# Laying q and k six tokens to a partition, and re-planning the first units, in a fused windowed-attention and gated-FFN kernel

## The chip, the cores and the metric

The kernel runs on one core of one Trainium2 chip. The core has a matrix engine (TensorE, PE in the profile, with its weight loads shown as PEld), VectorE (DVE), ScalarE (ACT), GpSimd (POOL), a queue engine (SP), and 16 DMA engines that move data between the chip's memory (HBM) and SBUF. TensorE writes its sums to PSUM banks, from which ACT or DVE must fetch them. The metric is the device time of one execution in microseconds (us); lower is better.

## The reference

Inputs in fp32: q, k and v of 8 batches x 8 heads x 576 tokens x 64, and three weights.

```python
scores = scale * np.matmul(q, k.transpose(0, 1, 3, 2))      # per batch and head, 576 x 576
rel = pos[:, None] - pos[None, :]
mask = (rel >= 0) & (rel < 64)                              # each token sees itself and the 63 before it
attn = softmax(where(mask, scores, -1e9)); x = attn @ v     # -> 4608 tokens x 512
gate = np.maximum(x @ w_gate, 0.0); val = x @ w_val         # 512 -> 1536
out = (gate * val) @ w_out                                  # 1536 -> 512, fp32
```

## The kernel before, in words

The attention is cut into 24 **units** of 192 tokens, three to a batch (all 8 heads at once); the FFN into 12 **tiles** of 384 tokens, two units each. Everything is multiplied in fp16.

*A unit's steps.* `u_cast` (L194) makes fp16 of fp32 q and k where they were loaded as fp32. `u_trans` (L205) turns them with 32x32 block transposes on DVE into kT and qT (head dimension on partitions). `u_st` (L244) computes scores, 32 matmuls on quarters of the array, into four PSUM banks `st`, one for each pair of heads. `u_exp` (L265) does four exponentials on ACT into `p`; `u_mask` (L270) multiplies them by the band mask on DVE (units 0 and 1 get the mask as a large negative bias instead: `u_bias`, L218, four matmuls a unit). `u_pv` (L275) multiplies by v. From unit 1 on it is the wide form (L294): v's tile holds 64 columns of ones beside each head's 64 columns of v, so that one matmul gives the weighted values and the row sums. `u_copy` (L310, ACT, two copies of 64x768) and `u_sum` (L320, DVE, two transposes of 64x768) take values and sums out of the PSUM tile `pv`. `u_back` (L331: reciprocal, transpose) and `u_norm` (L339: a product) write the fp16 input `xt` of the tile.

*A tile's steps.* `hidden` (L377): for each of 12 blocks f of 128 hidden columns, four matmuls with the gate weights wg, then four with the value weights wv (a "group" is four matmuls); ACT applies relu to the first into `r_sb` (L385), DVE multiplies that by the second into `g_sb` (L388). `output` (L426) or `output_by_rows` (L435): 36 matmuls with wo (L412), three copies by ACT (L419) and three stores issued by SP. The PSUM pool `f_ps` has four banks (tag `h`), shared in turn by the groups, the outputs and unit 0's `st` and `pv`. The pool `a_ps` is one tile of four banks, used in turn by every other `st` and `pv`.

*Loads.* q and k of batches 0 and 1 (units 0 to 5) come as fp32, in pieces of 32 partitions: each partition takes pairs of consecutive tokens, so that runs of 512 bytes are contiguous. `qk_load` (L159) issues them on SP, half of the first ones on ACT. Those of batch 1 are held back by `qk_gate` (L181), a memset on POOL. From batch 2 on, one `qk_load` for a whole batch issues eight DMAs on the POOL queue, which convert to fp16 on the way. v (`v_load`, L186, two DMAs a unit) and the weights (`w_load`, L132) always take the POOL queue and convert on the way. POOL also casts k and q of most units 2 to 5 and k of unit 0 (L203).

*What sets the order.* Nothing is reordered by a scheduler. `Weaver` (L16) is a heap of (time, function): attention steps and loads are entered by `plan_unit` (L347) with planned times, and issued into the engines' queues while `hidden` and `output` advance a clock by the ideal length of their matmuls. The planned times set only the *order* in each in-order engine queue; on the chip semaphores hold each instruction until its data is there. `ready(n)` issues planned steps until unit n-1 is normalized. DMAs on the POOL queue go round eight semaphores, so the ninth issue waits for the first landing, and so on.

*Order of the work* (L444 on): load k, then q; 22 matmuls on zeros (`heat`, L228); constants; units 0 and 1; tile 0 on 192 tokens for f 0 to 3, twice, then on 384 tokens for f 4 to 11; tile 1's first half on 192 tokens; tile 0's output; tile 1's second half; its output; then tiles 2 to 11, each with two later units woven in.

Of the kernel before, what the change touches and what calls it, by code (L numbers as in the profile page):

```python
# [42 lines left out]
def kernel(  # L43
# [10 lines left out]
    nc = tc.nc  # L54
# [24 lines left out]
    a_ps = ctx.enter_context(tc.tile_pool(name="a_ps", bufs=1, space=bass.MemoryType.PSUM))  # L79
# [13 lines left out]
    def constants():  # L93
        for kT in kTs:
            nc.vector.memset(kT[:, :, 0:64], 0.0)
        nc.vector.memset(v16s[0][0:64, 0], 0.0)
        for i in range(UB):
            nc.vector.memset(v16s[i][64 if i == 0 else 0:, 0, :, 64:128], 1.0)
            nc.vector.memset(v16s[i][:, 1, :, 64:128], 1.0)
        nc.vector.memset(ones, 1.0)  # L100
        nc.vector.memset(ones0, 1.0)
        nc.vector.memset(ones0[0:64], 0.0)
# [4 lines left out]
        for band, lo, hi in ((mask[:, 0], 64, -1), (mask[:, 1], 0, 63), (ident, 0, 0)):  # L107
# [9 lines left out]
        nc.vector.tensor_scalar(bias, mask, 30000.0, -30000.0, MUL, mybir.AluOpType.add)  # L117

# [11 lines left out]
    w_done = set()  # L130

    def w_load(wt, src, f0, f1):  # L132

        sr = src.rearrange("(c p) n -> p c n", p=128)
        if wt is wo:
            dst, part = wo[:, f0:f1], sr[:, f0:f1]
        else:
            ns = slice(128 * f0, 128 * f1)
            dst, part = wt[:, :, ns], sr[:, :, ns]
        nc.gpsimd.dma_start(dst, part)  # L140
        w_done.update((wt.name, f) for f in range(f0, f1))

    def w_need(wt, f):
        while (wt.name, f) not in w_done:
            W.pop()

# [3 lines left out]
    def qk_tiles(b):  # L150
        for name in ("k", "q"):
            direct = b >= 2
            nat = a_in.tile([128, 2, UB, 3, 128], FP16 if direct else FP32,
                            name=name + ("h" if direct else "n"), bufs=2)
            for i in range(UB):
                units.setdefault(UB * b + i, {})[name + ("16" if direct else "")] = nat[:, :, i]
                units[UB * b + i][name + "nat"] = nat

    def qk_load(b, blocks=None, names="kq", two=False):  # L159

        for name, src in (("k", k), ("q", q)):
            if name not in names:
                continue
            nat = units[UB * b + UB - 1][name + "nat"].rearrange("p h u m e -> p h (u m) e")
            for i in range(G):
                g = i // 2 + 2 * (i % 2)
                rows = slice(32 * g, 32 * g + 32)
                eng = nc.gpsimd if b >= 2 else nc.scalar if two and g >= G // 2 else nc.sync
                if blocks is None:
                    eng.dma_start(  # L170
                        nat[rows].rearrange("p h m e -> p (h m) e"),
                        src[b, 2 * g:2 * g + 2].rearrange("h (m i j) d -> i (h m) (j d)", i=32, j=2))
                else:
                    m0, m1 = blocks
                    for h in range(2):
                        eng.dma_start(  # L176
                            nat[rows, h, m0:m1],
                            src[b, 2 * g + h, 64 * m0:64 * m1].rearrange(
                                "(m i j) d -> i m (j d)", i=32, j=2))

    def qk_gate(b):  # L181

        for name in ("k", "q"):
            nc.gpsimd.memset(units[UB * b][name + "nat"].rearrange("p h u m e -> p (h u m) e")[:, :, 0:1], 0.0)
# [9 lines left out]
    def u_cast(u, name):  # L194
# [3 lines left out]
        c16 = d[name + "16"] = a_16.tile([128, 2, 3, 128], FP16, name=name + "16")  # L198
        src = d[name]
        if u < 3 and (u, name) not in ((0, "k"), (2, "k")):  # L200
# [334 lines left out]
```

The softmax here doesn't subtract the row's maximum and nothing guards it: scores larger than these inputs give would overflow.

## Time and profile before

| | us |
|---|---|
| median of three runs (range) | 351.43 (350.75 to 351.93) |
| the profiled execution: its time | 352.04 |
| its span, first to last instruction | 350.3 |
| busy: PE / DVE / ACT / POOL | 334.8 / 232.9 / 180.4 / 89.2 |
| first FFN matmul starts | 19.19 |
| tile 1's second half starts | 62.23 |
| tile 2's first group starts | 82.48 |
| last output copy starts | 346.55 |

The profile's page gives busy times by engine; the span in 40 slices of 8.76 us (PE busy tenths, the clock granted to TensorE in tenths, the share of DMA engines busy, GB/s that they moved, counted in bytes as they land); the chain of work that ended last, followed back from the end; and groups of like instructions with busy time, mean length, and idle time ahead of them with what ended it. The timeline lists instructions in order of time: start, length, engine, line, operation, and in brackets the idle time before it and who ended it. A run of matmuls is shown with its pipeline's depth, so the distance between starts, not the length, is its cost.

### The profile page before, as it was taken

What the parts mean: (1) busy time and instruction counts of PE and PEld (TensorE: products, weight loads), DVE (VectorE), ACT (ScalarE), POOL (GpSimd) and SP (SyncE); (2) the same over time, 40 slices, a digit from 0 to 9 for tenths busy, and PEclk for the clock granted to TensorE, in tenths of its full rate; (3) what the DMA queues carried; (4) which work ended last, traced back from release to release, by engine and by line L of the source; (5) the groups of instructions that cost most, each with busy time, mean ns of one, the idle gap of its engine ahead of it and who ended that gap; (6) DMA issues with size and microseconds to landing.
All of it is one profiled execution on the core that took longest, in us unless ns stands there. A gap on an engine that the chain in (4) does not pass through costs nothing.

```text
span 350.3 us, 7421 instructions
## 1 busy us (share of the span) xinstructions
PE 334.8 (96%) x2910; PEld 200.6 (57%) x2910; DVE 232.9 (66%) x432; ACT 180.4 (52%) x346; POOL 89.2 (25%) x129
## 2 busy tenths in 40 slices
PE   8579989999999999999999999999999999999995
PEld 3467674865555655655665664664664664664652
DVE  6487756697766766766766766766776777675430
ACT  2745552746565464465564564563663663663331
POOL 5944022835110710134120720216110100000000
PEclk9859999999999999999999999999999999999999
DMA  6999999999833992429615894409906501001002
GB/s 189 165 204 191 213 196 95 186 94 189 91 25 99 90 97 92 32 18 184 81 11 112 63 111 107 30 3 158 121 2 104 49 2 60 33 0 62 30 2 90
DMA packets 95508, 32.21 MB, mean 92 GB/s; under 512 B 76017, under 2 KB 90865, under 8 KB 95473
## 3 DMA queue, kind: packets, MB, share of 16 engines
q0 software_dynamic: 80048, 17.57, 57.5%
q1 hardware_dynamic: 13760, 13.38, 13.3%
q10 hardware_dynamic: 1664, 0.79, 0.8%
q8 instruction: 23, 0.38, 0.4%
q14 instruction: 13, 0.10, 0.1%
HBM read 39.85 MB, written 9.44 MB: 141 GB/s over the span
## 4 chain that ended last, share of the span: by engine, by line
PE 70%; DMA 13%; DVE 8%; issue 4%; POOL 3%; SPq 1%; ACT 0%; DVEq 0%; POOLq 0%
PE h L398 37%; PE op L412 24%; PE pv L303 5%; DMA kn<-in_k_dram 5%; DVE g_sb L388 5%; DMA wv<-in_moe_w_val_dram 4%; DMA qn<-in_q_dram 4%; PE st L256 3%; DVE sT L329 3%; SPq L176 1%; POOL v L192 1%; DVE rT L335 1%; POOL wg L140 1%; POOL k L203 0%; POOL wv L140 0%
## 5 line engine op out<-in xcount | busy, mean ns | idle before, releaser
L398 PE MATMUL h<-xt,wv 128*128 128x384 f16 (+1 forms) x640 | 121.4, 313 | 2.7 <-DVE g_sb L388 1.4
L398 PE MATMUL h<-xt,wg 128*128 128x384 f16 (+1 forms) x640 | 121.3, 313 | 2.7 <-DVE xt L343 1.1
L388 DVE TENSOR_TENSOR g_sb<-r_sb,h 128x384 f16<-128x384 f32 (+1 forms) x160 | 79.6, 508 | 63.8 <-PE h L398 54.0
L385 ACT ACTIVATE r_sb<-h 128x384 f32<-128x384 f32 (+1 forms) x160 | 72.8, 464 | 57.9 <-PE h L398 43.3
L412 PE MATMUL op<-wo,g_sb 128*128 128x512 f16 x432 | 95.8, 379 | 0.5 <-DVE g_sb L388 0.3
L398 PEld LDWEIGHTS <-wg 128*128 128x128 f16 x640 | 60.7, 99 | 38.7 <-issue 4.7
L398 PEld LDWEIGHTS <-wv 128*128 128x128 f16 x640 | 60.5, 99 | 35.5 <-DMA wv<-in_moe_w_val_dram 2.1
L192 POOL DMA_DIRECT2D v<-in_v_dram x48 | 40.7, 851 | 156.4 <-PE pv L303 153.7
L412 PEld LDWEIGHTS <-g_sb 128*128 128x128 f16 x432 | 42.2, 98 | 49.9 <-issue 1.1
L329 DVE STREAM_TRANSPOSE sT<-pv 64x768 f32<-64x768 f32 x46 | 45.1, 980 | 23.4 <-ACT xv L318 20.3
L268 ACT ACTIVATE p<-st 128x512 f16<-128x512 f32 x96 | 53.0, 609 | 11.1 <-PE st L256 10.3
L419 ACT COPY o_sb<-op 128x512 f32<-128x512 f32 x36 | 20.9, 587 | 64.9 <-PE op L412 64.9
L318 ACT COPY xv<-pv 64x768 f32<-64x768 f32 x46 | 36.5, 793 | 25.9 <-PE pv L303 13.6
L272 DVE TENSOR_TENSOR p<-p,mask 128x512 f16<-128x512 f16 x88 | 33.7, 421 | 5.9 <-ACT p L268 5.7
L303 PE MATMUL pv<-p,v 128*128 128x128 f16 x368 | 25.4, 223 | 1.9 <-ACT p L268 1.9
L303 PEld LDWEIGHTS <-v 128*128 128x128 f16 x368 | 23.3, 100 | 5.1 <-DMA v<-in_v_dram 2.0
L337 DVE STREAM_TRANSPOSE rs<-rT 128x768 f32<-128x768 f32 x24 | 23.5, 978 | 0.8
L343 DVE TENSOR_TENSOR xt<-xv,rs 128x768 f16<-128x768 f32 x23 | 21.8, 949 | 0.8 <-ACT xv L318 0.4
L256 PE MATMUL st<-qT,kT 32*128 32x128 f16 x768 | 15.5, 215 | 1.6 <-DVE qT L216 1.2
L256 PEld LDWEIGHTS <-kT 32*128 32x128 f16 x768 | 11.3, 92 | 9.0 <-issue 7.6
L170 POOL DMA_DIRECT2D kh<-in_k_dram x24 | 15.8, 672 | 0.0
L170 POOL DMA_DIRECT2D qh<-in_q_dram x24 | 15.8, 679 | 0.0
(48 smaller groups left out, 80.7 us busy)
## 6 DMA issues: line engine op xcount, KB each, us to landing
out_dram<-o_sb SPq DMA_DIRECT2D x36, 256.0 KB, 2.0
v<-in_v_dram POOLq DMA_DIRECT2D x40, 128.0 KB, 4.1
kh<-in_k_dram POOLq DMA_DIRECT2D x24, 144.0 KB, 5.4
qh<-in_q_dram POOLq DMA_DIRECT2D x24, 144.0 KB, 7.1
wo<-in_moe_w_out_dram POOLq DMA_DIRECT2D x3, 512.0 KB, 15.9
kn<-in_k_dram SPq DMA_DIRECT2D x12, 96.0 KB, 7.1
qn<-in_q_dram SPq DMA_DIRECT2D x12, 96.0 KB, 5.9
wg<-in_moe_w_gate_dram POOLq DMA_DIRECT2D x2, 512.0 KB, 13.3
```

The source lines that it names most:

```text
L170: eng.dma_start(nat[rows].rearrange("p h m e -> p (h m) e"), src[b, 2 * g:2 * g + 2].rearrange("h (m i j) d -> i (h m) (j d)", i=32, j=2))
L192: nc.gpsimd.dma_start(v16[p0:128, w, :, 0:64], v[b, :, k0 + p0:k0 + 128].rearrange("h p d -> p h d"))
L256: nc.tensor.matmul(d["st"][g][:, (2 * hh + w) * 128:(2 * hh + w + 1) * 128], kT[rows, hh, ks + 128 * w:ks + 128 * w + 128, dh], d["qT"][ro ...
L268: nc.scalar.activation(d["p"][g].rearrange("p h c -> p (h c)"), d["st"][g], ACT.Exp, scale=scale)
L272: nc.vector.tensor_tensor(p, p, mask.rearrange("p w c -> p (w c)")[:, None, :].to_broadcast([128, 2, 256]), MUL)
L303: nc.tensor.matmul(pv[:, g, e, 64 * w:64 * w + 128], v16[:, w, c0:c0 + 128], d["p"][g][:, e, 128 * w:128 * w + 128], start=(e == 0 and w = ...
L318: nc.scalar.copy(d["xs"][rows], d["pv"][rows, :, g, 0:U])
L329: nc.vector.transpose(to[64 * e:64 * e + 64], d["pv"][64 - 64 * e:128 - 64 * e, :, e, 0:U])
L385: nc.scalar.activation(r_sb[:, 0:n], h1[:, 0:n], ACT.Relu)
L388: nc.vector.tensor_tensor(g_sb[:, f, c0:c1], r_sb[:, 0:n], h2[:, 0:n], MUL)
L398: nc.tensor.matmul(h[:, 0:n], wt[:, c, f * 128:f * 128 + 128], xt[:, c, c0:c1], start=(c == 0), stop=(c == NC - 1))
L412: nc.tensor.matmul(op, g_sb[:, f, bass.ds(sub * 128, 128)], wo[:, f], start=(f == 0), stop=(f == NF - 1))
```

## The change

- **Layout of q and k.** `qk_load` now takes one unit, and lays six consecutive tokens of one head (1536 contiguous bytes in fp32) to a partition, 4 head pairs x 32 rows on 128 partitions, two DMAs for each of q and k. The transposes write with a stride of six tokens instead of two.
- **Who loads and casts.** Units 0 and 1 still come as fp32 on SP and ACT (8 DMAs); their casts are halves on DVE, two of them on ACT. Units 2 to 5, like all later ones, are loaded by the POOL queue with conversion on the way, one unit at a time, placed among v and the weights in order of use. POOL's eight casts, the memset gate and the remaining SP loads are gone.
- **POOL's first work.** The bands are made first, then v of units 0 and 1, then the weights in six pieces of 4 blocks (before: eight, the first four of 2 blocks). POOL no longer casts k of unit 0 ahead of them.
- **Constants.** The ones beside v, and one kT's zeros, are set on DVE later; unit 1 takes unit 0's form of `u_pv`, with separate ones.
- **Order.** `hidden` takes `each`: tile 0 issues four gate groups, then four value groups. Tile 0's output comes ahead of tile 1's first half. A weight's planned landing (`landed`) advances the plan's clock. Zero matmuls: 5 and 2 around unit 0's bias, 11 ahead of the first gate group. All planned times are new.
- **PSUM.** `a_ps` is two tiles of two banks; `u_copy` and `u_sum` work on halves: four copies and four transposes of 64x384 a unit.

```diff
-    a_ps = ctx.enter_context(tc.tile_pool(name="a_ps", bufs=1, space=bass.MemoryType.PSUM))
+    a_ps = ctx.enter_context(tc.tile_pool(name="a_ps", bufs=2, space=bass.MemoryType.PSUM))
...
+    def qk_load(u, names="kq", queues=None):
+
+        b, uu = divmod(u, UB)
         for name, src in (("k", k), ("q", q)):
             if name not in names:
                 continue
...
+            direct = queues is None
+            nat = a_in.tile([128, 2, 6 * D], FP16 if direct else FP32,
+                            name=name + ("16" if direct else "n"), bufs=4 if direct else 2)
+            units.setdefault(u, {})[name + ("16" if direct else "")] = nat
+            part = src[b, :, U * uu:U * uu + U].rearrange("(g h) (i j) d -> h g i (j d)", h=2, j=6)
+            for h in range(2):
+                (nc.gpsimd if direct else queues[h]).dma_start(nat[:, h], part[h])
...
+        c16 = d[name + "16"] = a_16.tile([128, 2, 6 * D], FP16, name=name + "c")
+        for h in range(2):
+            (nc.vector.tensor_copy if h or u else nc.scalar.copy)(c16[:, h], d[name][:, h])
...
-        nc.vector.transpose(dst.rearrange("p h (m i j) -> p h m j i", i=32, j=2), src)
+        nc.vector.transpose(dst.rearrange("p h (i j) -> p h j i", j=6), src)
...
+            halves = [a_ps.tile([128, 2, 512], FP32, name="st", tag="a") for _ in range(2)]
+            d["st"] = [halves[g // 2][:, g % 2] for g in range(G)]
...
+            for e in range(2):
+                rows = slice(64 * e, 64 * e + 64)
+                nc.scalar.copy(d["xs"][rows, 2 * g:2 * g + 2], d["pv"][g][rows, :, e, 0:U])
...
+            for e in range(2):
+                nc.vector.transpose(to[64 * e:64 * e + 64, 2 * half:2 * half + 2],
+                                    d["pv"][half][64 - 64 * e:128 - 64 * e, :, e, 0:U])
...
-        for f in range(f0, f1):
+        for fb in range(f0, f1, each):
+            r_sbs = {}
             for i, wt in enumerate((wg, wv)):
...
+                for f in range(fb, fb + each):
+                    W.advance(W.clock)
+                    w_need(wt, f)
...
+        qk_load(0, "k", (nc.sync, nc.scalar))
+        qk_load(0, "q", (nc.sync, nc.scalar))
+        qk_load(1, "kq", (nc.sync, nc.sync))
...
+        heat(5, units[1]["st"][0])
+        constants()
+        bands()
+        u_bias(0)
+        heat(2, units[1]["st"][0])
+        W.at(3.0, lambda: v_load(0))
+        W.at(3.1, lambda: v_load(1))
+        landed = 13.0
+        for f0 in (0, 4, 8):
+            for wt, src in ((wg, moe_w_gate), (wv, moe_w_val)):
+                W.at(3.2, lambda c=(wt, src, f0, f0 + 4, landed): w_load(*c))
+                landed += 2.6
+        W.at(12.0, lambda: qk_load(2))
+        W.at(12.2, lambda: v_load(2))
+        landed += 4.3
+        for f0 in (0, 4, 8):
+            W.at(18.0, lambda c=(wo, moe_w_out, f0, f0 + 4, landed): w_load(*c))
+            landed += 2.6
...
+        W.at(9.5, lambda: heat(11))
...
-        T = 72.2
+        T = 69.0
...
-        W.advance(18.8)
+        W.advance(12.6)
         ready(1)
-        hidden(0, 0, U, 0, 4)
+        hidden(0, 0, U, 0, 4, 4)
         ready(2)
-        hidden(0, U, TT, 0, 4)
-        hidden(0, 0, TT, 4)
+        hidden(0, U, TT, 0, 4, 4)
+        hidden(0, 0, TT, 4, NF, 4)
+        output_by_rows(0)
         ready(3)
         hidden(1, 0, U)
-        output_by_rows(0)
         ready(4)
         hidden(1, U, TT)
         output(1)
```

## The prediction, made before the changed kernel ran

> **What bounds the kernel now.** I read the 40 slices of the page first, to separate stages. Rows: PE, granted clock, DMA engines, GB/s.
>
> ```profile
> PE   8579989999999999999999999999999999999995
> PEclk9859999999999999999999999999999999999999
> DMA  6999999999833992429615894409906501001002
> GB/s 189 165 204 191 213 196 95 186 94 189 91 25 99 90 97 92 32 18 184 81 11 112 63 111 107 30 3 158 121 2 104 49 2 60 33 0 62 30 2 90
> ```
>
> From the eighth slice on PE is full and DMA soon mostly idle; before that PE has holes, the clock falls once, and DMA is busy without a break from 2 to 57 us. So the end is set by when PE reaches its steady run, and by that run's length. The chain that ended last, by time (start, length, what):
>
> ```profile
> 0.80 2.63 DMA kn<-in_k_dram
> 3.45 2.88 DMA qn<-in_q_dram
> 6.36 0.82 POOL k L203
> 7.19 3.38 POOL v L192 x4
> ...
> 14.21 14.51 DMA wv<-in_moe_w_val_dram
> ...
> 33.68 6.73 DMA kn<-in_k_dram
> 40.42 5.73 DMA qn<-in_q_dram
> 46.17 7.17 DMA kn<-in_k_dram
> ...
> 53.84 5.63 DMA qn<-in_q_dram
> 59.62 0.83 POOL q L203
> ```
>
> Up to 62 us it is loads: first q and k, then weights queued behind POOL's cast, then q and k of batch 1, until unit 4's scores at 61.1. After that it is PE. Two windows of the timeline show the throttle and a steady tile (PE and PEld busy, DVE, ACT, POOL, then clock, DMA share, GB/s):
>
> ```profile
> 20.00:25.00 5.00, 3.96 (x24) 3.40 (x25) 4.55 (x9) 3.16 (x6) 3.08 (x4) 0.50 1.30 205
> 109.40:136.10 26.70, 26.65 (x230) 15.44 (x229) 18.95 (x34) 14.52 (x27) 8.54 (x12) 1.00 0.80 92
> ```
>
> PE's lost time is countable. In the steady run a group of four 384-column matmuls starts every 0.652 us, an output matmul every 0.216, a unit's scores take 0.57 and its wide pv 0.89. A tile is 24 x 0.652 + 36 x 0.216 + 2 x 1.46 = 26.34 against a measured period of 26.72 (323.14 - 82.64 = 240.5 for nine). The surplus of 0.38 has one visible part, after an even unit's pv: groups start at 120.52 and 121.39, 0.22 late, behind a DVE that had waited 1.90 us for ACT's copies of the same PSUM tile before its own transposes. From 19.19 to 82.64, tiles 0 and 1 with units 2 to 5 need 53.0 us by those rates (groups on 192 columns 0.332); they took 63.45.
>
> **The change, step by step.**
>
> *Bytes ahead of the weights.* By the 5-us windows, 9.40 MB had landed by 48.5 us, when the last wo piece did (issued at 29.9, 18.6 to landing). The same point of the new order needs q, k of units 0, 1 in fp32 (1.57 MB), v of units 0 to 2 (0.72), weights (4.72), and q, k of unit 2 in fp16 (0.39): 7.40 MB. Rates: q, k alone with 512-byte runs ran at 248 GB/s (2 to 8 us); three 256 KB stores of 2 KB rows at 313 to 383 (62 to 64 us); weights at 205; v, after taking out the fp32 beside it at 248, at about 117 from 9 to 15 us, and the mix of v and later q, k at 150. The new 1536-byte runs are in no row: between 248 and 355 GB/s, 6.3 to 4.4 us; I take 5.0, nearer the stores by size of run. A layout that bought nothing would cost 1.3 us more.
>
> The Trainium skill's "DMA: Bandwidth & Descriptors", Specifications, speaks against that part: it puts line rate at transfers of at least 512 bytes, which the old runs already are, so the wider runs would gain nothing and the sum would be 1.3 us larger; the trace has 248 against 313 to 383 on either side of that size, though for loads against stores.
>
> *First weights.* POOL is free after its bands at 3.15 instead of 7.13 (its cast waited for q). Its four v issues at 0.70 to 0.89 and six weight issues at 0.78 are then done by about 11, so data, not issue, sets landings. DMA starts at 2.2: + 5.0 (q, k) + 4.0 (v of two units, 0.46 MB at 117) + 2.56 (512 KB at 205): first wg at 13.8, last wv at 26.5; unit 2's q, k and v 4.2 more (fp16 q, k at 205, or at worst at the 152 that the old 256-byte landings had from 65 to 70 us); wo at 33.3, 35.9, 38.4. The difference way, 2.0 MB fewer at 205 to 340, gives 38.7 to 42.6. I take 39.
>
> *First matmul.* Unit 0's q, k land by 5.5; cast half 0.5 (128x768 took 0.83), transposes 2 x 0.58, scores at 6.4, 4 exponentials of 0.6, pv by 9.7 if v is there (issued 4 us sooner; it took 3.4 to 6.0 to land), then copies and sums by quarters, reciprocal 0.30, transpose 0.98, product 0.96: 12.7 to 13.5. So wg decides: **13.8 instead of 19.19, 5.4 us earlier**. The casts moved to DVE are six halves, 0.4 to 0.55 each, on a DVE that idled 4.5 of the first 10 us in the trace; POOL's eight at 0.83 go. Transposes with a wider write stride: 0.58 each, at worst double; that bound is +1.2 us a unit, covered by DVE's idle 7.8 us a steady tile, uncovered in the first two units.
>
> *Clock.* It fell to 0.50 at 15.4 and came back at 25.4, though PE had stood still at most 1.9 us at a time; eight groups of 0.332 took 6.5 us there. In the new order, matmuls on zeros (11 x 0.216) fill the wait for wg. The 22 zero matmuls at the start, now 7, cost nothing either way: PE waits for q there. I count the clock as staying up; if not, 2 to 3 us, part of them hidden behind wo's landing.
>
> The Trainium skill's "TensorE: Matmul & The Clock Gate", Part 1, asks for a whole idle window of some 3.4 us before the clock halves; by that rule no hole of the old start would have done it and the new filling would be needless, while the trace shows a fall with holes of 1.0 and 1.9 us in a third-busy stretch.
>
> *Tile 0.* Four gate groups first mean that PE needs only wg at 13.8 and wv at 16.4; before it waited 0.8 and 0.5 us for wv pieces. Its value groups end with the last wv, about 31; unit 2's scores need its q, k (28.9) and transposes, its pv its masks: about 34.5. Output by rows takes 7.8, and its last third 2.6 after the last wo: **max(42.3, 41.6), 42**.
>
> *Tile 1, first half.* PE needs 24 x 0.332 + 1.46 for unit 3 = 9.4, and 0.6 until the first output bank is copied; DVE needs more: 12 products of 0.35, masks 1.7, sums 2.2, back and norm 2.2, transposes 1.2, together 11.5, and 0.2 until the first. **42 + 11.7: it ends at 53.7; before, at 62.23: 3.1 us more gained.** Unit 1's narrow pv (32 matmuls, about 1.1 by unit 0's, for 16 wide at 0.89) falls in the wait for wv. Unit 3's q, k (after wo, 41) and unit 4's (45) are no longer last; DVE is.
>
> *Tile 1, second half and output:* 20.4 before, 9.42 of them needed for its groups and two attention steps but 11.25 taken, by DVE. The same work; sums that start on one PSUM half while ACT copies the other: 0.5 less.
>
> *Halves in the steady run.* DVE loses its wait of 1.9 us ahead of each even unit's sums, but has four transposes of 64x384 for two of 0.98. By the 128x384 ones (0.55) four are 2.2, 0.24 more a unit; ACT's copies, from 2 x 0.79 to 4 x about 0.46, 0.25 more. Ends: the 0.22 stall goes (-2.0 over nine tiles), or four cost 0.98 each, as much as a whole one (+1.96 a unit). I take -0.1 a tile, **0.9**. More POOL issues (four for a unit instead of eight for three, 0.67 to 0.89 each) are free: POOL waited 154 us for pv. A v load still holds the POOL queue until pv of three units before is done, with the next unit's q, k behind it; those are planned 24 us ahead of use, and land in 5 to 7. Memsets moved to about 20 us (six of 0.49) lie where DVE has 0.35 us of product for each 0.66 of PE. The end is untouched.
>
> **Sum.** 5.4 + 3.1 + 0.5 + 0.9 = 9.9; 352.04 - 9.9 = 342.1 for the profiled execution, which stood 0.6 above its median: **341.5**.
>
> **Rivals.**
> - *The start pays half.* The clock falls again, v holds back pv, or DMA is no faster on wide runs (+1.3, +2 to 3, and DVE's surplus in both halves of tile 1): 4 lost, **345.5**. For: DVE is over PE there by my own count. Against: wo hides some.
> - *The surplus vanishes too.* The steady stall goes whole (-1.1 beyond my count) and tile 1 runs near PE's need (13.8 + 53.0 + 1.1 for unit 1's pv = 67.9 to tile 2, against my 73.6; half of that): **337.5**. Against: ACT and DVE both fill that stretch.
> - *Slower: the half transposes cost a fixed time.* At 0.98 each, DVE has 1.96 us more in the burst after each unit's pv, and PE's four banks wait on its products: 0.22 becomes about 1.7 a tile, +13.5 over nine, **356**. It decides above +1.0 us a tile, where the start's 9.0 us are eaten. Against: 128x384 takes 0.55, 128x768 0.98, so cost goes with columns.
>
> **Chances.** Forecast 0.57, half 0.20, vanishing surplus 0.13, slower 0.07, no change 0.03 (start and steady run cancelling). 0.3% is about what a measurement of this kernel can tell from no change. Range 337 to 347: the second and third cases lie in it with the ends of q, k's rate and the landings; the slower case is left out. Faster by over 0.3%: 0.90 (the first three), within: 0.03, slower: 0.07.
>
> **What would show it.** First wg group near 13.8; clock 1.00 from 15 to 25 us; last wo near 39; tile 2's first group at 73 to 74 instead of 82.5; steady period 26.6; sums of 64x384 near 0.55. I am wrong if tile 0's output matmuls still wait for wo after 42, if the clock row shows a 5 in slices 2 or 3, or if the period exceeds 27.

## The result, and the profile after

The changed kernel took **360.89 us** (median of four runs, 360.00 to 363.22) against 351.09 (350.61 to 351.93) for the kernel before on the same chip: ratio 1.029, 95% interval 1.023 to 1.034. It is slower by 2.9%. The forecast was 341.5, in a range that ended at 347, so the time lies outside it and on the other side of the kernel before. The profiled execution took 360.0 us, its span is 358.2.

The same four rows of the page of 40 slices (8.96 us each here): PE, granted clock, DMA engines, GB/s.

```profile
PE   5339999899999999999999999999999999999995
PEclk9568999999999999999999999999999999999999
DMA  8997999979876595596587586487578521001002
GB/s 97 213 197 94 115 178 104 195 70 110 118 68 38 126 76 47 109 75 45 120 66 49 118 73 54 107 72 58 114 61 73 106 15 60 31 0 60 29 3 89
```

PE reads 5, 3, 3 in the first three slices, where it was 8, 5, 7; the clock has a 5 in slice 2 and a 6 in slice 3. The first slice moved 97 GB/s, where the kernel before moved 189, though its DMA digit is 8 where it was 6. That last pair is the thing to notice: a higher DMA share than before, half the bytes (the windows of 1 us further on take the two apart). The chain that ended last, by time (start, length, what):

```profile
3.06 2.16 SPq L168
5.27 3.67 SPq L168
8.98 15.46 DMA qn<-in_q_dram
```

The chain starts with SP itself standing for 2.16 and 3.67 us at issues of q and k loads (its first two issues took 0.72 and 0.70), then 15.5 us of one q load. The long DMA pieces of batch 1 are gone from it, as forecast; a q load has taken their place, some 25 us earlier. PE's timeline has the consequences (start, length, engine, line, operation, idle time before and its cause):

```profile
15.07 1.04 PE L237 MATMUL st<-qT,kT 32*128 32x128 f16 x32 [8.83 <-DVE qT L197]
25.77 1.04 PE L237 MATMUL st<-qT,kT 32*128 32x128 f16 x32 [5.54 <-DVE qT L197]
26.75 4.21 PE L215 MATMUL h<-zero 128*128 128x512 f16 x11
30.79 0.49 PE L388 MATMUL h<-xt,wg 128*128 128x192 f16 x4
```

Unit 0's scores start at 15.07 (I had 6.4), unit 1's at 25.77, the first gate group at 30.79 (13.8; before, 19.19). From tile 2 on, all is well: a steady period is 26.50, clock 1.00, in the row of the windows that answers to the 26.70 of before.

```profile
20.00:25.00 5.00, 0.23 (x8) 0.16 (x5) 1.04 (x4) 0.00 (x0) 0.72 (x1) 0.83 1.29 222
92.25:118.75 26.50, 26.50 (x228) 15.46 (x228) 22.18 (x40) 14.62 (x30) 8.91 (x12) 1.00 0.73 77
```

| starts at, us | before | forecast | after |
|---|---|---|---|
| first gate group | 19.19 | 13.8 | 30.79 |
| tile 1's second half | 62.23 | 53.7 | 72.33 |
| tile 2's first group | 82.48 | 73.6 | 92.25 |
| from there to the end of the span | 267.8 | 266.8 | 265.95 |

The whole loss lies before tile 2: 9.8 us later than before, 18.65 later than forecast.

### The profile page after: what moved, and what is told of

Read it like the earlier page. It is cut to its first block, busy times and chain, and to the rows that moved or that the text cites. A ratio compares the mean times of both kernels' runs of the same rounds, so it can differ in the third digit from the quotient of the medians.

```text
span 358.2 us, 7528 instructions
## 1 busy us (share of the span) xinstructions
PE 334.2 (93%) x2922; PEld 199.5 (56%) x2922; DVE 253.1 (71%) x485; ACT 185.2 (52%) x392; POOL 111.3 (31%) x157
## 4 chain that ended last, share of the span: by engine, by line
PE 86%; DMA 5%; SPq 2%; DVE 2%; ACT 2%; issue 2%; POOL 1%; ACTq 0%; POOLq 0%
PE h L388 52%; PE op L402 24%; PE pv L288 5%; DMA qn<-in_q_dram 4%; PE st L237 4%; SPq L168 2%; PE h L215 1%; DMA v<-in_v_dram 1%; ACT r_sb L373 1%; DVE xt L331 0%; DVE qT L197 0%; POOL q L168 0%; DVE g_sb L376 0%; ACT xv L300 0%; ACT xv L304 0%
## 5 line engine op out<-in xcount | busy, mean ns | idle before, releaser
L388 PE MATMUL h<-xt,wg 128*128 128x384 f16 (+1 forms) x640 | 118.2, 310 | 2.6 <-DVE xt L331 1.5
L388 PE MATMUL h<-xt,wv 128*128 128x384 f16 (+1 forms) x640 | 118.4, 310 | 0.5 <-ACT r_sb L373 0.5
L373 ACT ACTIVATE r_sb<-h 128x384 f32<-128x384 f32 (+1 forms) x160 | 74.1, 466 | 62.4 <-PE h L388 52.3
L176 POOL DMA_DIRECT2D v<-in_v_dram x48 | 41.9, 877 | 143.3 <-PE pv L288 128.7
L316 DVE STREAM_TRANSPOSE sT<-pv 64x384 f32<-64x384 f32 x88 | 51.1, 580 | 12.4 <-PE pv L288 11.1
L304 ACT COPY xv<-pv 64x384 f32<-64x384 f32 x88 | 41.6, 473 | 16.0 <-DVE sT L316 9.1
L168 POOL DMA_DIRECT2D k<-in_k_dram x44 | 31.4, 715 | 10.5 <-DMA v<-in_v_dram 4.9
L168 POOL DMA_DIRECT2D q<-in_q_dram x44 | 29.4, 673 | 6.4 <-DMA k<-in_k_dram 2.6
L288 PE MATMUL pv<-p,v 128*128 128x128 f16 x352 | 23.6, 219 | 0.9 <-ACT p L249 0.5
L288 PEld LDWEIGHTS <-v 128*128 128x128 f16 x352 | 21.5, 98 | 4.1 <-issue 1.3
```

The costliest lines, as they stand in the source:

```text
L168: (nc.gpsimd if direct else queues[h]).dma_start(nat[:, h], part[h])
L176: nc.gpsimd.dma_start(v16[p0:128, w, :, 0:64], v[b, :, k0 + p0:k0 + 128].rearrange("h p d -> p h d"))
L288: nc.tensor.matmul(d["pv"][g // 2][:, g % 2, e, 64 * w:64 * w + 128], v16[:, w, c0:c0 + 128], d["p"][g][:, e, 128 * w:128 * w + 128], star ...
L304: nc.scalar.copy(d["xs"][rows, 2 * g:2 * g + 2], d["pv"][g][rows, :, e, 0:U])
L316: nc.vector.transpose(to[64 * e:64 * e + 64, 2 * half:2 * half + 2], d["pv"][half][64 - 64 * e:128 - 64 * e, :, e, 0:U])
L373: nc.scalar.activation(r_sb[:, 0:n], h1[:, 0:n], ACT.Relu)
```

## The experiments

Theory formed on the trace above: the new q, k loads use only four of the sixteen DMA engines. Rivals: the wide rows are slow by themselves; SP's issues are slow; POOL's queue holds them up. The row that suggests four engines is in the windows of 1 us (DMA share and GB/s are the last two columns), the changed kernel:

```profile
2.00:3.00 1.00, 1.00 (x4) 0.33 (x3) 0.14 (x2) 0.44 (x1) 0.86 (x4) 1.00 0.13 22
3.00:4.00 1.00, 1.00 (x4) 0.33 (x3) 0.23 (x1) 0.99 (x2) 1.00 (x3) 1.00 0.21 60
4.00:5.00 1.00, 1.00 (x4) 0.35 (x3) 0.00 (x0) 0.05 (x1) 1.00 (x2) 1.00 0.27 100
```

Only SP's and ACT's loads run here, but for three packets of v at the end of the third window (from 5 us on v joins, and the share reads 1.05). The share climbs to 0.27 (0.27 x 16 = 4.3 engines) at 100 GB/s. In the kernel before the share was 1.01, 0.85, 1.00 in these windows. The new source pattern is [4 head pairs, 32 rows, 384 elements]; the old loads had 32 partitions outermost. The Trainium skill's "DMA: Bandwidth & Descriptors", in the section on why a DMA increments its semaphore by 16, has the rule: a DMA is spread over the largest number of engines up to 16 that divides the slowest dimension larger than 1 of both patterns. With 4 outermost that is 4, with 32 it is 16. The prediction cited that page, and not that rule.

### How many engines: 16, 4, 2, and 4 in the kernel before

**k16**: the changed kernel with its fp32 loads cut so that 32 rows are outermost; the same bytes, runs and layout, 4 DMAs instead of 2 for each of q and k.

```diff
+            if not direct:
+                for g in range(G):
+                    (nc.gpsimd if direct else queues[g % 2]).dma_start(
+                        nat[32 * g:32 * g + 32],
+                        src[b, 2 * g:2 * g + 2, U * uu:U * uu + U].rearrange("h (i j) d -> i h (j d)", j=6))
+                continue
```

> The changed kernel with one thing altered: the fp32 loads of units 0 and 1 are cut by rows instead of by heads (four DMAs of 32 partitions x 2 x 1536 bytes for each of q and k), so that the outermost dimension of the source is 32 rows, not 4 head pairs; bytes, length of runs, layout in SBUF and queues stay. Few engines (theory): with the source's outermost dimension 4, a load ran on 4 of the 16 DMA engines (the engines' share of 0.21 to 0.27 and 60 to 100 GB/s from 3 to 5 us), and everything else had to wait for those four; cut by rows, the share from 3 to 5 us is above 0.8, unit 0's scores start before 8 us, the first gate group before 16 us, and the time is 341 to 346. Crowding (rival 1: v and weights, issued 4 us earlier, take the DMA engines from q and k) or slow wide runs (rival 2: 1536-byte runs move slower): nothing alters, first gate group at 28 to 31 us, 358 to 362.

**k2**: as many DMAs, but cut so that 2 is outermost.

```diff
+            if not direct:
+                for gg in range(2):
+                    for h in range(2):
+                        queues[h].dma_start(nat[64 * gg:64 * gg + 64, h], part[h][2 * gg:2 * gg + 2])
+                continue
```

> The changed kernel with the same number of DMAs as the one cut by rows, but each fp32 load of units 0 and 1 cut into two pairs of head pairs, so that the source's outermost dimension is 2. Few engines: 2 of 16 engines, a share near 0.13 and about 50 GB/s from 3 to 5 us, 1.57 MB take over 30 us, first gate group after 40 us, 371 to 380. Crowding or slow wide runs: bytes and runs are those of the changed kernel, first gate group at 28 to 31, 358 to 362.

**before_k4**: the kernel before, its batch 0 loaded with the 4 head pairs outermost, 512-byte runs as they were.

```diff
...
+                            for m in range(m0, m1):
+                                (nc.scalar if two and i else nc.sync).dma_start(
+                                    units[UB * b + UB - 1][name + "nat"].rearrange("p h u m e -> p h (u m) e")[:, i, m],
+                                    src[b, :, 64 * m:64 * m + 64].rearrange("(g h) (i j) d -> h g i (j d)", h=2, j=2)[i])
...
```

> The kernel before with one thing altered: the fp32 loads of batch 0 keep their 512-byte runs, layout and order, but go as 128-partition DMAs, one for each block and half of the heads, whose source has the 4 head pairs outermost (36 issues for 32). Few engines: a share near 0.25 from 3 to 5 us, unit 0's scores at 17 to 20 us instead of 10.7, weights later by as much since POOL's cast waits for q, 358 to 363. Crowding: POOL still issues nothing before q is there, so 351 to 353. Slow wide runs: runs are as before, 351 to 353.

| q, k loads | us | ratio to before (95%) |
|---|---|---|
| k16 | 350.26 | 0.997 (0.995 to 0.998) |
| after: 4 engines | 360.89 | 1.029 (1.023 to 1.034) |
| k2 | 388.67 | 1.107 (1.104 to 1.110) |
| before_k4 | 379.2 | 1.079 (1.077 to 1.081) |

The trace of k16 that is read from here on is that of a second run of the same kernel, **k16_look** (350.28).

> The kernel with the fp32 loads cut by rows once more, for a trace of an undisturbed execution (the earlier trace fell in an execution whose matmuls ran at about a quarter of the usual rate throughout). Few engines repaired: share above 0.8 from 2 to 5 us, unit 0's scores before 9 us. Time 350. The 18 us by which the changed kernel reached tile 2 later than forecast should be seen to shrink by only 9 to 10, and what takes the other 9 should show ahead of the first gate group: either DVE, whose queue has unit 1's casts (waiting for unit 1's q) ahead of unit 0's sums, or the landing of the first wg piece.

The three windows in k16_look; then one window of k2, and of its next but one the rows of SP's and ACT's queues (packets, MB, share of 16 engines); then a longer window in before_k4:

```profile
2.00:3.00 1.00, 1.00 (x4) 0.32 (x3) 0.14 (x2) 0.32 (x1) 0.86 (x4) 1.00 0.99 287
3.00:4.00 1.00, 1.00 (x4) 0.34 (x3) 0.23 (x1) 0.99 (x2) 1.00 (x3) 1.00 0.98 238
4.00:5.00 1.00, 1.00 (x4) 0.32 (x3) 0.41 (x1) 0.62 (x2) 1.00 (x2) 1.00 1.00 249
```

```profile
3.00:4.00 1.00, 1.00 (x4) 0.33 (x3) 0.23 (x1) 0.00 (x0) 1.00 (x3) 1.00 0.07 28
```

```profile
q1 hardware_dynamic: 16, 0.02, 6.6%
q10 hardware_dynamic: 16, 0.02, 6.5%
```

```profile
2.00:10.00 8.00, 7.45 (x29) 2.96 (x27) 3.61 (x12) 1.49 (x2) 2.20 (x6) 1.00 0.26 76
```

The share is 1.0 with 32 outermost and 0.27 with 4. With 2 it reads 0.07 in the first windows, little more than one engine of sixteen (0.06), and from 5 to 6 us SP's and ACT's queues have 13.1% together, 2.1 engines, in which 32 packets of 1536 bytes are about 49 GB/s. The time follows. k16 and k2 differ in nothing but the cut: 38 us. Runs of 512 bytes with 4 outermost are as slow (0.26, 76 GB/s), so neither the width of the runs nor SP's issuing is the cause. k2 and before_k4 lost more than I had expected; in before_k4 batch 1 is issued behind batch 0 in SP's queue, from 48.01 us on, and the clock stayed at 0.50 from 15 to 55 us. So **10.6 us of the 19 (360.9 to 350.3) are the four engines**. Of the theory's signs in k16 the share came true, and unit 0's scores all but did (8.07 for before 8); the first gate group (21.18 for before 16) and the time (350.3 for 341 to 346) did not. That k16 only ties with the kernel before leaves 8.8 us to the forecast.

**k16all**: the POOL queue's q, k loads cut by rows as well (`if True` in place of `if not direct`).

> Loads cut by rows for every unit, those on the POOL queue too (8 issues a unit for 4, about 2.7 us of POOL more a unit). If the POOL loads with 4 head pairs outermost also ran on few engines and delayed what came with them: median landing of k and q below 5.5 us for 6, tile 0's wo earlier, 346 to 349. If several of them in flight spread over all engines anyway: 350 to 351, or 352 if POOL's issue time now holds the queue.

349.91, ratio 0.996 (0.995 to 0.997): within the interval of k16. How POOL's q, k loads are spread has no worth that these runs can tell.

### The halves of PSUM alone

**before_halves**: the kernel before with `a_ps` as two tiles, copies and sums by halves, and the changed kernel's steady plan times; its loads and start untouched.

```diff
-    a_ps = ctx.enter_context(tc.tile_pool(name="a_ps", bufs=1, space=bass.MemoryType.PSUM))
+    a_ps = ctx.enter_context(tc.tile_pool(name="a_ps", bufs=2, space=bass.MemoryType.PSUM))
...
-        plan_unit(2 * t + 1, T + 13.2, tr=late, norm=(6.0, 6.9, 7.8, 8.8))
+        plan_unit(2 * t + 1, T + 13.2, tr=late, copy=(4.7, 5.8), norm=(4.8, 5.9, 6.9, 8.0))
```

> The kernel before with one part of the change alone: two PSUM tiles of two banks for st and pv, copies and sums by halves, and the changed kernel's planned times for them in the steady run. If the halves are what shortened the steady period from 26.72 to 26.50 us, the period is 26.5 and the time 349 to 350 (nine tiles at 0.22). If the period came from elsewhere (loads one unit at a time, later loads of v), it stays at 26.7 and the time at 351.

349.17, ratio 0.994 (0.993 to 0.996); a tile in the steady run, and the row sums' group in before and in this kernel (count, busy, mean ns, idle before and its cause):

```profile
94.00:120.51 26.51, 26.51 (x230) 15.46 (x229) 19.76 (x39) 15.20 (x31) 8.36 (x12) 1.00 0.55 66
```

```profile
L329 DVE STREAM_TRANSPOSE sT<-pv 64x768 f32<-64x768 f32 x46 | 45.1, 980 | 23.4 <-ACT xv L318 20.3 <-PE pv L303 2.6
```

```profile
L332 DVE STREAM_TRANSPOSE sT<-pv 64x384 f32<-64x384 f32 x92 | 53.4, 580 | 13.1 <-PE pv L303 11.8
```

The period is 26.51 as in after (26.50), with none of the other parts. The half transposes cost 0.58, not a fixed 0.98, and the 20.3 us of waiting for ACT's copies are gone (DVE's idle time ahead of them fell from 23.4 to 13.1 us, most of it now a wait for PE). This part of the change is good by itself, worth 2 us.

### What else is late at the start

In k16_look, DVE and then PE between 14 and 21 us:

```profile
14.56 0.63 DVE L190 CAST qc<-qn 128x384 f16<-128x384 f32 x2 [2.45 <-DMA qn<-in_q_dram]
15.22 0.85 DVE L203 STREAM_TRANSPOSE qT<-qc 128x384 f32<-128x384 f32 x1
15.94 0.59 DVE L319 STREAM_TRANSPOSE sT<-pv 128x192 f32<-128x192 f32 x2
```

```profile
16.13 1.04 PE L243 MATMUL st<-qT,kT 32*128 32x128 f16 x32 [4.87 <-DVE qT L203]
17.10 4.24 PE L221 MATMUL h<-zero 128*128 128x512 f16 x11
21.18 0.49 PE L394 MATMUL h<-xt,wg 128*128 128x192 f16 x4
```

Unit 1's q is cast only at 14.56. Unit 0's sums stand behind that cast in DVE's queue, though its value products ran from 9.61 to 11.2. In this trace the clock falls in the hole of 4.87 us, and the eleven zero products take 4.1 us (17.10 to 21.18) instead of 2.4. Three suspects, then: DVE's order, the clock, and whatever makes that q late.

**k16_order**: unit 1's steps planned 3 us later and its casts 4 to 5, behind unit 0's sums.

```diff
-        plan_unit(1, 9.0, (6.3, 7.5), (-1.8, -0.6), 1.3, None, 4.3, (5.7, 5.8, 5.9, 6.0), (5.6, 5.2, 6.2, 7.1), 0.5)
+        plan_unit(1, 12.0, (11.3, 11.3), (-0.6, -0.5), 1.3, None, 4.3, (5.7, 5.8, 5.9, 6.0), (5.6, 5.2, 6.2, 7.1), 0.5)
```

> Loads cut by rows, and unit 1's casts, transposes and later steps planned 3 us later, so that on DVE unit 0's sums, reciprocal and product come ahead of the casts that wait for unit 1's q. Wait in the queue (theory): unit 0's product ends near 14 us instead of 20, the first gate group starts at about 16 (first wg piece), and the time is 345 to 348. Weights decide (rival): the first gate group is early, but PE then waits for wv and wo pieces as before and the time stays at 349 to 351.

352.34, ratio 1.005 (1.002 to 1.008): missed. The first gate group did move to 19.01, but unit 1's casts were now behind unit 0's work, its product ended at 26.03, and PE waited 2.82 for it with the clock down again. DVE's order only chooses which unit is late.

**k16_noheat**: no eleven zero products (`W.at(9.5, lambda: heat(11))` removed).

> The change with q,k of units 0 and 1 cut by rows (350.3 us), and without the eleven zero products ahead of unit 1's value products. In the run with them they stood on TensorE from 17.10 to 21.18 at a granted clock of 0.50, though unit 1's exponentials ended near 19.3 and tile 0's first tokens were ready at 20.1. Theory 'the warming products stand in the way': the first gate group starts near 20.2 instead of 21.2, unit 1's value products near 19.4 instead of 21.6, tile 0's second half 1 to 2 us sooner, in all 348.3 to 349.5. Theory 'they are what brings the clock back': without them the clock is at 0.50 past 24, the first gate groups take twice 0.7 us each, and the run ends at 350.5 to 353.

351.19, ratio 0.999 (0.998 to 1.000). The first gate group came 0.1 us sooner, at 21.05, but ran at the low clock (4 matmuls in 0.74 instead of 0.33), which lasted to 25: tile 2 started at 83.93 instead of 82.61. By the medians (351.19 against 350.26) the zero products are worth about 0.9 us, as the second theory had it. The trace alone would not show it: unit 1's q was cast at 15.20 in it instead of 14.56, and in traces with the same loads in the same order that cast moved between 13.83 (k16_warm) and 15.20.

**k16_warm**: eighteen more zero products, and unit 1's bias, in the hole.

```diff
-        W.at(6.1, lambda: u_bias(1))
+        W.at(8.95, lambda: heat(18, units[1]["st"][0]))
+        W.at(8.97, lambda: u_bias(1))
```

> The change with q,k cut by rows (350.3 us), with eighteen more zero products and unit 1's bias product between unit 0's value products and unit 1's scores, so that TensorE's hole from 11.2 to 16.1 is filled (18 x 0.213 = 3.8 us); nothing else moves. It asks what the fallen clock costs by itself, which the forecast counted as nothing. Theory 'the clock is a part of the miss': it stays at 1.00 through 13 to 20, the eleven zero products take 2.4 instead of 4.2 us, the first gate group starts near 20.1 instead of 21.2 and the time is 348.8 to 349.6. Theory 'only the late tokens count': the first gate group stays at 21 and the time within 0.4 us of 350.3.

350.15, ratio 0.996 (0.995 to 0.998). The clock was up from 14 us on, the eleven took 2.4 us again, and in that trace tile 2 started at 81.78 instead of 82.61, though q, too, was cast 0.7 us sooner, at 13.83; the median does not tell it from k16. The fallen clock costs under 1 us here: the hole matters for what is missing in it.

**k16_pairs**: tile 0's gate and value groups in turn again, the `4` of `each` left out of the three `hidden(0, ...)`.

> Loads cut by rows; tile 0 takes gate and value groups in turn again instead of four gates ahead of four values. If gates ahead of values saves waits for wv pieces: 351 to 353. If tile 0 is not held by wv pieces, because it starts late: 350 as with the loads cut by rows alone.

349.58, ratio 0.994 (0.992 to 0.996): "gates ahead of values" buys nothing here; the weights are not what tile 0 waits for.

### Why unit 1's q is late

**k16_early**: unit 1's loads on the queues of SP and ACT in turn.

```diff
-        qk_load(1, "kq", (nc.sync, nc.sync))
+        qk_load(1, "kq", (nc.sync, nc.scalar))
```

> The change with q,k of units 0 and 1 cut by rows (350.3 us), unit 1's loads issued on the queues of SP and ACT in turn instead of SP alone, so that the last is issued near 5.5 instead of 7.4. Theory 'unit 1's q is late because it is issued behind SP's other loads, into the stretch in which v's short rows fill the engines' (163 GB/s from 8 to 12 against 250 to 290 from 2 to 5): its cast starts near 12 instead of 14.56, unit 0's sums near 13.5 instead of 15.94, the hole of TensorE from 11.2 to 16.1 shrinks to some 2.5 us, and the run ends at 347.5 to 349. Theory 'the engines are full whatever the order of issue': q of unit 1 lands within 1 us of 14.5 and the time stays within 0.8 us of 350.3. Against both: the four issues on ACT push the first exponential's table load and unit 0's casts back by 1 to 2 us, 351 to 352.

**348.52**, ratio 0.993 (0.990 to 0.995). q's cast moved to 13.21, the first gate group to 18.97, as the first theory had it, though the third happened too: ACT stood at its issues, and the load of its table began at 6.79 instead of 2.68.

**k16_early_dve** puts ACT's issues behind that table load, and all of unit 0's casts on DVE.

> As the run with unit 1's loads on both queues (348.5 us), with ACT's share of them issued behind the table load and with all of unit 0's casts on DVE. In that run ACT stood at its last issues until 6.79, its casts of unit 0 began at 8.19 instead of 4.56 and unit 0's scores at 10.78 instead of 8.07, and it gained 1.8 us all the same. Theory 'two chains start tile 0, and both count': unit 0's scores start near 8.5, the casts of unit 1's q stay near 13.2, and since unit 0's sums still stand behind those casts on DVE the first gate group moves by less than 1 us (18 to 19): 347.6 to 348.6. Theory 'unit 0's late scores are what is left': the first gate group moves with the scores, by 2 us or more, to about 16.7, and the time to 346 to 347. Against both: if TensorE's hole now falls between unit 0's product at 11 and unit 1's scores at 14.8, the clock falls in it as it did at 13 in the run with SP alone, and the time is 349.5 to 350.5.

350.0, ratio 0.995 (0.993 to 0.997): by the medians nearly all of the gain was gone, though the two intervals overlap. With ACT's issues later, unit 1's k was cast at 13.05 and q at 14.96. That fits "it is when these loads are *issued* that counts" (q at 13.21 and 13.74 in the two runs that issue it early, at 13.83 to 15.20 in seven others with v and weights beside it), but the ranges all but meet, so it is not shown. **k16_best** (early, no eleven zero products, groups in turn) and **k16_best2** (early_dve, groups in turn) gave 349.52 and 349.6, no better than their parts.

> The change with q,k of units 0 and 1 cut by rows, unit 1's loads on both queues, no eleven zero products, and tile 0's gate and value groups in turn. If lateness of unit 1's q and the warming products each cost what the two runs beside it are expected to show: 346.5 to 348, below the kernel before by 3 to 5 us. If the clock falls without the products: 350 to 352.

> As the run with unit 1's loads on both queues and unit 0's casts on DVE, with tile 0's gate and value groups in turn, which by themselves moved 350.3 to 349.6. If the two add, 0.7 us below the run beside it: 346.9 to 347.9. If groups in turn only help where the clock was down, no difference to it within 0.5 us.

Next, what shares the engines with q and k. **k16_nov**: v of units 0 and 1 not loaded.

```diff
-        W.at(3.0, lambda: v_load(0))
-        W.at(3.1, lambda: v_load(1))
+        W.at(3.0, lambda: nc.gpsimd.memset(v16s[0][64:128, 0, :, 0:64], 0.5) and None)
+        W.at(3.05, lambda: nc.gpsimd.memset(v16s[0][:, 1, :, 0:64], 0.5) and None)
+        W.at(3.1, lambda: nc.gpsimd.memset(v16s[1][:, :, :, 0:64], 0.5) and None)
```

> The change with q,k of units 0 and 1 cut by rows (350.3 us), in which v of units 0 and 1 is not loaded but filled with a constant by GpSimd (so the output of the first 384 tokens differs). Leaves out 0.46 MB in four loads of short rows, whose issues took GpSimd 3.5 us. It asks what the missing 7 us at the start are. Theory 'the loads crowd each other': unit 1's q lands near 10 instead of 14.5, the first weights near 10 instead of 15.8, the first gate group starts near 15 and the whole run ends near 344 to 345.5. Theory 'order on DVE and the clock': q lands earlier by at most 2 us and the time stays above 348.

350.2, ratio 0.995 (0.993 to 0.997), and unit 1's q was still cast at 14.13: v is not needed for the lateness, since the weights were then issued from 5.18. **k16_hold** does the opposite: v stays, and GpSimd makes half of unit 1's casts ahead of the weights, so that these wait.

```diff
+            (nc.gpsimd.tensor_copy if h and u else nc.vector.tensor_copy if h or u else nc.scalar.copy)(c16[:, h], d[name][:, h])
...
-                W.at(3.2, lambda c=(wt, src, f0, f0 + 4, landed): w_load(*c))
+                W.at(7.6, lambda c=(wt, src, f0, f0 + 4, landed): w_load(*c))
```

> The change with q,k of units 0 and 1 cut by rows (350.3 us), in which GpSimd makes the second half of the casts of unit 1's k and q (DVE made both), ahead of its six weight loads: the weights are issued only when unit 1's q has landed. Without v's loads that q still landed at 14.1, with the weights issued from 5.2 on; so if anything crowds it, the weights do. Theory 'the weights crowd unit 1's q': it lands at 9 to 10.5, unit 0's sums on DVE follow at 11.5, TensorE's hole shrinks to about 1 us and the clock stays up, the first weights land near 14 to 15 and the first gate group starts there or at 15 to 16 instead of 21.2, and the time is 344.5 to 347. Theory 'the loads of q,k are slow by themselves': q lands at 13 or later, the weights follow from there, the first gate group starts past 21 and the time is 351 to 354. Against the first, too: the weights come late for tile 0's second and third four groups (needed some 5 and 10 us after the first), 347 to 349.

350.0, ratio 0.997 (0.995 to 0.998), and q was cast at 13.88. Taken alone, each run spoke for "slow by themselves". **k16_hold_pairs**, with groups in turn, gave 350.57, the same within 0.7.

> As the run beside it, with tile 0's gate and value groups in turn. If the weights are now the bound of tile 0 (a gate piece and a value piece of 512 KB in 2.5 us each), four gates ahead of four values need the value piece 2.6 us later than groups in turn do, and this run is slower by 0.5 to 2 us. If not, it is the same within 0.7 us.

**k16_alone** does both at once, so that q and k have the engines to themselves.

> The run with the weights held back and the run without v's loads put together: q,k cut by rows, weights issued only when unit 1's q has landed, v of units 0 and 1 filled with a constant (the output of the first 384 tokens differs). So q,k are alone on the sixteen engines until they have landed. With v beside them unit 1's q landed at 13.9, with the weights beside them at 14.1. Theory 'loads on different queues share the engines, so unit 1's q, the last of its queue, ends with whatever runs beside it': alone it lands near 9 (issued by 7.4, 1.57 MB at the 250 GB/s of the first microseconds from 2.2 on gives 8.5), TensorE's hole is under 1 us and the first gate group is bound by the weights alone, at 16 to 18; the time 345 to 347.5. Theory 'q,k are slow by themselves': it lands past 12 all the same, and the time is 349 to 351.

**345.91**, ratio 0.984 (0.982 to 0.986). Windows, DVE and PE of k16_alone:

```profile
2.00:8.00 6.00, 4.32 (x10) 1.23 (x9) 3.58 (x8) 2.51 (x4) 2.98 (x7) 1.00 0.84 236
10.00:12.00 2.00, 1.85 (x63) 1.34 (x58) 1.55 (x4) 1.29 (x4) 2.00 (x3) 1.00 0.27 9
```

```profile
9.45 0.59 DVE L190 CAST qc<-qn 128x384 f16<-128x384 f32 x1
```

```profile
11.29 0.64 PE L243 MATMUL st<-qT,kT 32*128 32x128 f16 x32
11.86 2.55 PE L221 MATMUL h<-zero 128*128 128x512 f16 x11
15.92 0.50 PE L394 MATMUL h<-xt,wg 128*128 128x192 f16 x4 [1.51 <-DMA wg<-in_moe_w_gate_dram]
```

q is cast at 9.45 instead of 14.56, PE has no hole ahead of unit 1's scores, the clock stays up, and the weights alone hold the first gate group, at 15.92. So loads of different queues do share the engines (with v and weights beside them, k16_look moved 154 GB/s at a share of 2.27 from 8 to 12 us), and **either v or the weights is enough** to make the last of q, k late by 4 to 5 us. The Trainium skill's "DMA: Bandwidth & Descriptors", section "Issuing engines are not separate DMA queues", says that DMAs issued by the scalar, sync or gpsimd engine run on the same 16 engines and interleave; the traces agree (q at 9.45, 13.88, 14.13 and 14.56 with nothing, v, the weights, and both beside it). The 4.35 us that k16_alone gained on k16 are not all to be had by an order of issue: k16_alone leaves v's 0.46 MB out, and no run loads everything and keeps q and k alone.

## Why the prediction was wrong

By tile 2's first group, where 18.65 us were lost:

| step of the sum | us | shown by |
|---|---|---|
| q, k on four engines | 9.6 | 92.25 to 82.61, k16_look |
| v and weights beside q, k (v not loaded at all) | 3.9 | 82.61 to 78.72, k16_alone |
| first weights land later than counted | 2.1 | 15.92, k16_alone, against 13.8 |
| tile 0 | 0.9 | 29.14 (15.92 to 45.06) against 28.2 |
| tile 1, first half | 2.1 | 13.76 (45.06 to 58.82) against 11.7; 1.0 of it a wait for unit 3's q, k in k16_alone only |

- **"Between 248 and 355 GB/s ... I take 5.0" is the step that failed.** I priced the new loads by bytes and by size of run, and both ends of my range took all sixteen engines for granted. The loads ran at 22 to 100 GB/s, and the last q landed at 24.4 us (8.98 + 15.46), 22.2 after the start at 2.2 instead of 5.0. No row of before could price this, but the diff shows the pattern, and the page that the prediction cites has the rule. On sixteen engines, alone, the last q landed at 9.17 (k16_alone), 7.0 us after 2.2, later even than my 6.3. The 1536-byte runs made 236 GB/s (2 to 8 us in k16_alone), against 248 for the 512-byte runs of before: the wide rows bought nothing. There the rule that I weighed (line rate from 512 bytes on) fits, and my reading of the stores does not.
- **"5.0 + 4.0 + 2.56: first wg at 13.8"** lined up transfers one after the other. They run side by side, and what is needed first ends late: in k16_look the first weights, issued at 6.56 beside all the rest, landed 9.2 us later, at 15.8. An addend was missing too: in k16_alone, which holds them back on purpose, the first weights were issued at 9.85, 9 GB/s moved from 10 to 12, and the group that waited for them started 6.1 us after the issue; I had 2.56.
- **"First matmul ... so wg decides"** held in k16_alone. In after and k16_look unit 1's q decided, through DVE's in-order queue: a step I had put with those that are covered.
- **"I count the clock as staying up"** was wrong in after (0.50 from 10 to 15 us, 0.83 from 20 to 25). In k16_warm filling the hole was worth under 1 us; what the fall cost in after was not measured. The zero products are worth 0.9 us (k16_noheat).
- **"Four gate groups first mean that PE needs only wg"**: no worth shown (k16_pairs, k16_hold_pairs). **Tile 0** itself was well sized: 28.5 us to tile 1 in after and in k16_look, 28.2 forecast.
- **Tile 1, first half**, was 13.0 in after and in k16_look. "0.2 until the first" product is the term that failed: ACT's three output copies come ahead of its first relu, and DVE's first product starts 1.6 us into the stretch. DVE's work was sized well (10.6 us busy against 11.5), but it stood idle for 2.4.

```profile
51.31 0.35 DVE L382 TENSOR_TENSOR g_sb<-r_sb,h 128x192 f16<-128x192 f32 x1 [2.91 <-ACT r_sb L379]
```

  The line is from k16_look, where the stretch starts at 49.70. "Tile 1, second half": 19.9 forecast, 19.9 measured; no run shows whether the 0.5 in it came from the halves.
- **Transposes "0.58 each, at worst double"**: 0.85. The groups of before and after:

```profile
L216 DVE STREAM_TRANSPOSE kT<-kh 128x384 f32<-128x384 f32 x18 | 10.0, 554 | 0.0
```

```profile
L197 DVE STREAM_TRANSPOSE kT<-k 128x384 f32<-128x384 f32 x22 | 18.8, 856 | 0.0
```

  The cover held in the steady run: the period fell all the same.
- **Halves**: 0.58 for 64x384 against "near 0.55", and the rival with a fixed 0.98 is out. The gain was 1.9 us from tile 2 to the end where I counted 0.9: the stall of 0.22 went whole, as the second rival had it, without the "0.1" that I kept back.

My slower rival named the wrong mechanism. The case that came about, loads that lose engines, was in none of them: "DMA is no faster on wide runs" was as bad as I let it be.

## What to carry to other kernels

Before pricing a load in GB/s, read the outermost dimension of both its access patterns: a layout with better runs can leave twelve of sixteen DMA engines idle, and the profile shows it as a DMA share that stands at a fraction (0.27 here) while nothing holds the loads back. Transfers issued on different queues in the same microseconds slowed each other here, the ones needed first too (q at 9.45 alone, at 13.9 to 14.6 beside others), so ask of each load what else will be in flight with it. Among these versions the best complete one was k16_early (348.52), with before_halves (349.17) inside its interval.

## What the runs showed of the hardware

- With the same 1536-byte runs, four engines moved 100 GB/s (4 to 5 us in after), two about 49 (worked out from SP's and ACT's 32 packets of 1536 bytes from 5 to 6 us in k2), sixteen 238 to 287 (2 to 5 us in k16_look): about 25 GB/s an engine on four and on two, 15 to 18 on sixteen.
- A 32x32 block transpose of 128x384 took 0.55 us when it wrote pairs (two tokens apart) and 0.85 with six tokens between: the wider write stride went with half as much again.
- The granted clock in a window is not the whole of it. In k16_look PE stood still from 6.2 to 8.07, and unit 0's scores then took 0.64. In k16_early it stood still from 6.2 to 10.78, and the same scores took 1.04, as unit 1's did in k16_look at 16.13 under a clock of 0.50; yet the clock reads 1.00 in every window of k16_early's start. The lengths of the matmuls say that it had fallen there.

```profile
8.07 0.64 PE L243 MATMUL st<-qT,kT 32*128 32x128 f16 x32 [1.85 <-DVE qT L203]
```

```profile
10.78 1.04 PE L243 MATMUL st<-qT,kT 32*128 32x128 f16 x32 [4.56 <-DVE qT L203]
```

- Nor did the clock follow the holes from one trace to the next. k16_pairs gives PE the same work as k16_look up to the first gate group, but there the scores took 1.00 at 8.17, after a hole of 2.56 us, and the clock read 0.50 from 9 to 11 us and 1.00 from 12 to 15, where k16_look's read 1.00 to 13 us and then fell. What decides it stayed open.
